# Fused score tiles accumulated in parts, and matmuls on zeros ahead of the first load: talking-heads attention and a squared-ReLU feed-forward in one kernel

## Chip, cores and metric

The kernel runs on one core of one Trainium2 chip. The metric is the device time of one execution in microseconds (us). Before the change the median of three runs is 600.85 us (600.27 to 602.12). One execution more was profiled; it took 600.99 us, and its trace, from the first instruction to the last, spans 599.2 us. Engines are named as in the profile: PE is TensorE (matmuls), PEld its weight loads, DVE VectorE, ACT ScalarE, POOL GpSimd, and SP the engine whose queue issues most DMAs.

## What is computed

Eight batches, 12 heads, 448 positions, head size 64. Scores are mixed over the heads before the softmax, and the attention weights are mixed again after it. The result is the input of a feed-forward of 768 to 2048 to 768 with a squared ReLU.

```python
scores = scale * np.matmul(q, k.transpose(0, 1, 3, 2))
scores = np.einsum('bhij,hg->bgij', scores, w_pre)
scores = scores - np.max(scores, axis=-1, keepdims=True)
attn = np.exp(scores)
attn = attn / (np.sum(attn, axis=-1, keepdims=True) + 1e-09)
attn = np.einsum('bhij,hg->bgij', attn, w_post)
attn_out = np.matmul(attn, v)
x = attn_out.transpose(0, 2, 1, 3).reshape(B * S, H * D)
h = np.maximum(x @ w_in, 0.0)
out = h * h @ w_out
```

## The kernel before, in words

**Tiles and steps.** A step is one tile: 10 query positions (`IQ`) of one batch with all 12 heads, 120 rows (`RG`). A batch has 45 tiles (`NT`), so there are 360 steps. At step i, `mix` (L369) makes the mixed scores of tile i in a PSUM bank `m_ps`, ACT takes the exp with its row sum (L384), DVE the reciprocal (L386), POOL the scaled second mixing matrix `pn` (L388). Four steps later (`LAG`) `unmix` (L392) multiplies the exps with `pn` on PE (L401), and DVE copies the result to `at` (L403). Between these, feed-forward units fill PE's time.

**Two ways to a mixed tile.** From tile 12 of batch 0 on, the plain scores of 120 or 128 queries, a block, are made by a burst (`score_burst`, L320): for each of the pairs of heads two matmuls into `s_ps` banks (L332), copied to the S tile by ACT (L342) or DVE (L344). There are two S tiles, so a block overwrites the one of two blocks before. `gather` (L349) then brings the rows of 10 queries with all heads together in a G tile with a DMA on SP's queue (L361), and one matmul of `mix` (L381) mixes the heads. The first 12 tiles of batch 0 (`FUSED`) have no S: there `mix_queries` (L172) has multiplied the turned queries with the mixing weights on DVE (L176; the products, named `w` in the profile, lie in the room of the later w_out weights), and `mix` makes the tile with six accumulating matmuls (L376), one for each pair of heads.

**The start.** q and k of batch 0 come in three loads each of four heads (q0, k0, q1, k1, q2, k2 below), issued on POOL's queue (L83), then v. `turn_unit` (L181) turns four heads with 16 transposes on PE (L193) and one copy (L195): queries on DVE, keys on ACT. For each unit u the order is: turn q, mix the first `NEAR` = 4 tiles' queries and then the other eight, turn k. After unit 1 the burst of pairs 0 and 1 of block (0,0) is made (in the order written). Pairs 2 and 3 follow in step 0, pairs 4 and 5 in step 1. From step 2 (`GATHERS_AT`) two gathers a step are written, from tile 12 on, until all 12 tiles of the block are gathered; then one a step, 10 tiles ahead (`AHEAD`). Some gathers bring the next block's bursts along: those of tiles 17 and 20 the bursts of block (0,1), those of tiles 29 and 32 (steps 19 and 22) those of block (0,2), which takes the S tile of block (0,0).

**What sets the order.** PE's and POOL's instructions run in the order of the program (`manual_schedule`, L425). On ACT, DVE and SP a scheduler orders them when the kernel is built. All eight PSUM banks are one pool: `tr_ps`, `s_ps`, `m_ps`, `at_ps`, `h_ps`, `o_ps` and `ot_ps` take one each and give it back when it has been read.

**Loads at steps.** POOL issues the loads of weights and of the next batches at fixed steps, each ahead of that step's `pn`: w_in at -1, 1, 3, 18, 21 and 24 (`W1_AT`), batch 1's k and q at 5, 7, 9, 11, 13 and 15 (`KQ_AT`).

```python
if h % 2 == 0 or (b == 0 and h in ((1, 3) if blk == 0 else (3, 9))):
    nc.scalar.copy(out=sb[:, h, :], in_=ps[:, 0:S])
```

The two lines (L341) share a burst's copies out: of block (0,0)'s 12 copies ACT makes eight.

Of the kernel before, what the change touches and what calls it, by code (L numbers as in the profile page):

```python
# [8 lines left out]
BF16 = mybir.dt.bfloat16  # L9
# [5 lines left out]
B, H, S, D = 8, 12, 448, 64  # L15
DMODEL = H * D
DFF = 2048
NPAIR = H // 2
# [3 lines left out]
IQ = 10  # L22
NT = 45
RG = H * IQ
FUSED = 12
FQ = FUSED * IQ
NEAR = 4
STARTS = {0: (FQ, 2 * FQ, S - 128)}
FIRST = {0: (FUSED, 2 * FUSED, 3 * FUSED)}
BURSTS = {0: ([5, 8], [5, 8], [3, 6])}  # L30
for _b in range(1, B):
    STARTS[_b], FIRST[_b], BURSTS[_b] = (0, 128, 256, 384), (0, 13, 26, 39), ([5, 8], [5, 8], [6], [0, 3])
GATHERS_AT = 2
HALF = H // 2
TT = 15
TQ = TT * IQ
# [14 lines left out]
def kernel(  # L51
# [11 lines left out]
    nc = tc.nc  # L63
    P = nc.NUM_PARTITIONS

    consts = ctx.enter_context(tc.tile_pool(name="consts", bufs=1))
# [7 lines left out]
    def bank(name, dtype=F32):  # L74
        return psp.tile([P, 512 if dtype == F32 else 1024], dtype, name=name, tag="ps")
# [6 lines left out]
    def load(t, src, b, h0=0, h1=H):  # L82
        nc.gpsimd.dma_start(out=t[0:PR, h0:h1, :, :].rearrange("p h r d -> p h (r d)"),  # L83
                            in_=src[b, h0:h1, :, :].rearrange("h (p r) d -> p h (r d)", r=R))

    staged, vs = {}, {}
    staged[0] = (stage_tile("qst", 1), stage_tile("kst", 1))
# [41 lines left out]
    for t in range(3 * P // IQ, NT):  # L129
        n0, n = max(0, 3 * P - IQ * t), min(IQ, S - IQ * t)  # L130
# [29 lines left out]
    for t in ets:  # L160
# [4 lines left out]
    w2 = [wts.tile([P, FT // 4, DMODEL], BF16, name=f"w2_{x}") for x in range(4)]  # L165

    qTs, kTs, xts, h2ts, ats = {}, {}, {}, {}, {}

    qmix = [w2[u][:, :, :].rearrange("p c m -> p (c m)")[:, 0:2 * FQ * H].rearrange(
        "p (y t g i) -> p y t g i", y=2, g=H, i=IQ) for u in range(NPAIR // 2)]  # L170

    def mix_queries(u, t0, t1):  # L172

        for y in range(2):
            qs = qTs[0][:, 2 * u + y, IQ * t0:IQ * t1].rearrange("p (t i) -> p t i", i=IQ)
            nc.vector.tensor_tensor(out=qmix[u][:, y, t0:t1, :, :],  # L176
                                    in0=qs.unsqueeze(2).to_broadcast([P, t1 - t0, H, IQ]),
                                    in1=wrep[:, 2 * u + y, :, :].unsqueeze(1).to_broadcast([P, t1 - t0, H, IQ]),
                                    op=ALU.mult)
# [41 lines left out]
    def load_v(b, x):  # L221
        if x == 0:
            vs[b] = stage_tile("v", 2)
        load(vs[b], v, b, 4 * x, 4 * x + 4)
# [121 lines left out]
    def rows_of(t):  # L346
        return H * min(IQ, S - IQ * t)

    def gather(s):  # L349
# [16 lines left out]
            x += n  # L366
        Gs[s] = g

    def mix(s):  # L369
        n = rows_of(s[1])  # L370
        b, t = s
        ps = bank("m_ps")
        fused = b == 0 and t < FUSED
        if fused:
            for p in range(NPAIR):
                nc.tensor.matmul(ps[0:n, 0:S], rhs=kTs[b][:, p, :],  # L376
                                 lhsT=qmix[p // 2][:, p % 2, t, :, :].rearrange("p g i -> p (g i)"),
                                 start=(p == 0), stop=(p == NPAIR - 1))
        else:
            m = pres[max(x for x in pres if x <= t)] if b else pre  # L380
            nc.tensor.matmul(ps[0:n, 0:S], lhsT=m[0:n, 0:n], rhs=Gs.pop(s)[0:n, :], start=True, stop=True)  # L381
        e = ets[(NT * s[0] + s[1]) % ND]
        sm = work.tile([P, 1], F32, name="sm", tag="sm", bufs=4)
        nc.scalar.activation(out=e[0:n, 0:S], in_=ps[0:n, 0:S], func=ACT.Exp, scale=SCALE, accum_out=sm[0:n, 0:1])  # L384
        rc = work.tile([P, 1], F32, name="rc", tag="rc", bufs=4)
        nc.vector.reciprocal(out=rc[0:n, :], in_=sm[0:n, :])  # L386
        pn = work.tile([P, RG], BF16, name="pn", tag="pn", bufs=LAG + 2)
        nc.gpsimd.tensor_scalar(out=pn[0:n, :], in0=(post_gi if fused else post)[0:n, :], scalar1=rc[0:n, 0:1], scalar2=1.0,  # L388
                                op0=ALU.mult, op1=ALU.mult)
        esb[s] = (e, pn)  # L390
# [20 lines left out]
    def at_step(i, unit):  # L411
        timed.setdefault(i, []).append(unit)
# [10 lines left out]
    blocks = [(b, blk) for b in range(B) for blk in range(len(STARTS[b]))]  # L423
    steps = [(b, t) for b in range(B) for t in range(NT)]
    with tc.manual_schedule(engines={PE, POOL}):  # L425
        for x in range(3):
            load_v(0, x)
        for u in range(NPAIR // 2):
            turn_unit(0, 0, u)
            mix_queries(u, 0, NEAR)  # L430
            mix_queries(u, NEAR, FUSED)
            turn_unit(0, 1, u, nc.scalar.copy)
            if u == 1:
                score_burst(0, 0, [0, 1])
        loads = {}
        ahead = [FUSED]

        def at_load(i, f, *args):
            loads.setdefault(i, []).append(lambda: f(*args))

        for x in range(3):
            at_load(V1_AT[x], load_v, 1, x)
        for x in range(6):
            at_load(KQ_AT[1][x], load_qk, 1, x)
            at_load(KQ_AT[2][x], load_qk, 2, x)
        for x, i in enumerate(W1_AT):
            at_load(i, load_w1, x)
        for x, i in enumerate(W2_AT):
            at_load(i, load_w2, x)
        for b in range(1, B):  # L450
            if b + 2 < B:
                for x in range(6):
                    at_load(NT * b + (30 if b == 1 else 22) + 2 * x, load_qk, b + 2, x)
            if b + 1 < B:
                for x in range(3):
                    at_load(NT * b + 34 + 2 * x, load_v, b + 1, x)
        def begin(units):
            owed[0] = max(owed[0], 0.0)
            filler.extend(units)

        for x, third, q0, q1 in EARLY:
            at_step(x, (0, lambda third=third, q0=q0, q1=q1: begin(ffn1_third(third, q0, q1))))
        bounds = sorted({x[0] for x in EARLY} | {FFN2_AT, 2 * NT + 1 + LAG})
        end = len(steps) + LAG + 3
        for i in range(-1, end):
            for f in loads.get(i, []):
                f()
            if i < 0:
                continue
            if i == NT // 2:  # L470
                for (_, n), (t, order) in orders.items():
                    half_pre(n, t, order)
            s0 = steps[i] if i < len(steps) else None
            s1 = steps[i - LAG] if LAG <= i < len(steps) + LAG else None
            if s0:
                b, t = s0
                if t == 0:
                    if b + 1 < B:
                        for x, u in enumerate(turn_units(b + 1)):
                            at_step(i + TURN.get(b, TURN[B])[x], u)  # L480
            early = [x for x in bounds if x > i]
            rest = early[0] - i if early else (1 + LAG - i) % NT + 1
            rest = min(rest, end - i) if i > len(steps) - NT // 2 else rest
            share = sum(w for w, _ in filler) / rest / 2
            now = timed.pop(i, [])
            if s0:
                mix(s0)
            for w, f in now:
                f()
                owed[0] -= w  # L490
            fill(share)
            if s1:
                unmix(s1)
                b1, t1 = s1
                if t1 % TT == TT - 1:
                    for u in av_units(b1, t1 // TT):
                        at_step(i + 3, u)
                if t1 == NT - 1:
                    at_step(i + 3 if b1 else FFN2_AT, (0, lambda b1=b1: filler.extend(ffn_units(b1))))
            if i < 2:  # L500
                score_burst(0, 0, [2 + 2 * i, 3 + 2 * i])
            for _ in range(2 if i >= GATHERS_AT else 0):
                if ahead[0] > min(max(i + AHEAD, 2 * FUSED - 1), len(steps) - 1):
                    break
                b2, t2 = steps[ahead[0]]
                gather((b2, t2))
                ahead[0] += 1
                blk2 = max(x for x in range(len(FIRST[b2])) if FIRST[b2][x] <= t2)
                nxt = blocks.index((b2, blk2)) + 1
                first = BURSTS[b2][blk2]  # L510
                if nxt < len(blocks) and t2 - FIRST[b2][blk2] in first:
                    x = first.index(t2 - FIRST[b2][blk2])
                    score_burst(*blocks[nxt], [3 * x, 3 * x + 1, 3 * x + 2])
            if i + 1 < end:
                fill(share)
        for j in sorted(timed):
            for _, f in timed[j]:
                f()
        fill(1e12)
# [30 lines left out]
```

## Time and profile before

| what | value |
|---|---|
| median of three runs | 600.85 us |
| profiled execution, and its span | 600.99 us, 599.2 us |
| DVE, ACT, POOL busy, of the span | 69%, 64%, 54% |
| granted clock, mean of the span | 0.995 |
| PE idle before its first matmul | 7.12 us |
| L376, the fused tiles' matmuls, 24 to 40 us | x42, 355 ns each |
| L401 (unmix), whole span | x1440, 216 ns each |
| L251 and L295 (feed-forward), whole span | x960, 315 ns; x768, 326 ns |
| gathers (G<-S), 105.0 KB | x284 |
| DMA, mean over the span | 121 GB/s |

The spans of matmuls overlap, since they are pipelined; a row "x6" in the timeline gives the length of six together. An engine's idle time counts where the chain that ended last goes through it. Each digit of the page's slices is a fortieth of the span, 15 us; DMA stands for how busy the core's 16 DMA engines were:

```profile
PEclk9999999999999999999999999999999999999999
DMA  9898999698569755795458855697544755431003
GB/s 128 141 199 164 191 197 196 128 172 193 100 101 140 145 100 109 121 156 124 98 94 135 151 111 101 113 143 138 109 79 69 133 119 107 84 50 54 27 27 79
```

### The profile page before, as it was taken

What the parts mean: (1) busy time and instruction counts of PE and PEld (TensorE: products, weight loads), DVE (VectorE), ACT (ScalarE), POOL (GpSimd) and SP (SyncE); (2) the same over time, 40 slices, a digit from 0 to 9 for tenths busy, and PEclk for the clock granted to TensorE, in tenths of its full rate; (3) what the DMA queues carried; (4) which work ended last, traced back from release to release, by engine and by line L of the source; (5) the groups of instructions that cost most, each with busy time, mean ns of one, the idle gap of its engine ahead of it and who ended that gap; (6) DMA issues with size and microseconds to landing.
All of it is one profiled execution on the core that took longest, in us unless ns stands there. A gap on an engine that the chain in (4) does not pass through costs nothing.

```text
span 599.2 us, 17220 instructions
## 1 busy us (share of the span) xinstructions
PE 574.3 (96%) x6011; PEld 372.2 (62%) x6011; DVE 411.7 (69%) x1044; ACT 380.6 (64%) x1105; POOL 326.1 (54%) x708
## 2 busy tenths in 40 slices
PE   4979999899999999999999999999999999999996
PEld 3547777566566666566565665666665666666553
DVE  5668769988767777767777777777867667666011
ACT  3757978676876557864776547775677547762410
POOL 5354897362777227862569316792377325761730
PEclk9999999999999999999999999999999999999999
DMA  9898999698569755795458855697544755431003
GB/s 128 141 199 164 191 197 196 128 172 193 100 101 140 145 100 109 121 156 124 98 94 135 151 111 101 113 143 138 109 79 69 133 119 107 84 50 54 27 27 79
DMA packets 88279, 72.28 MB, mean 121 GB/s; under 512 B 6688, under 2 KB 83200, under 8 KB 88192
## 3 DMA queue, kind: packets, MB, share of 16 engines
q1 hardware_dynamic: 50394, 48.16, 36.6%
q0 software_dynamic: 37216, 22.81, 29.3%
q8 instruction: 47, 0.77, 0.5%
q10 hardware_dynamic: 582, 0.21, 0.2%
q14 instruction: 40, 0.33, 0.1%
HBM read 45.70 MB, written 11.01 MB: 95 GB/s over the span
## 4 chain that ended last, share of the span: by engine, by line
PE 81%; DMA 10%; ACT 3%; issue 2%; DVE 1%; POOL 1%; SPq 1%; ACTq 0%; POOLq 0%; DVEq 0%
PE o_ps L295 24%; PE h_ps L251 22%; PE at_ps L401 10%; PE m_ps L381 10%; DMA G<-S 7%; PE ot_ps L209 6%; PE s_ps L332 4%; PE tr_ps L193 3%; ACT e L384 2%; DMA w<-in_moe_w_in_dram 2%; DMA kst<-in_k_dram 1%; ACT S L342 1%; PE m_ps L376 1%; DVE S L344 1%; PE s_ps L338 1%
## 5 line engine op out<-in xcount | busy, mean ns | idle before, releaser
L403 DVE CAST at<-at_ps 112x480 bf16<-112x480 f32 x360 | 228.5, 650 | 73.3 <-PE at_ps L401 72.8
L384 ACT ACTIVATE e<-m_ps 120x448 bf16<-120x448 f32 x360 | 195.5, 547 | 98.8 <-PE m_ps L381 92.4
L388 POOL TENSOR_SCALAR pn<-post,rc 120x120 bf16<-120x120 bf16 x348 | 129.0, 372 | 207.1 <-DVE rc L386 147.6
L251 PE MATMUL h_ps<-xt,w 128*128 128x448 bf16 (+2 forms) x960 | 169.6, 315 | 1.1 <-ACT hr L257 0.6
L295 PE MATMUL o_ps<-w,h 128*128 128x384 bf16 x768 | 138.7, 326 | 0.3 <-ACT S L342 0.2
L401 PE MATMUL at_ps<-pn,e 120*128 120x120 bf16 (+1 forms) x1440 | 135.1, 216 | 0.7 <-POOL pn L388 0.5
L401 PEld LDWEIGHTS <-e 120*128 120x128 bf16 (+1 forms) x1440 | 103.9, 98 | 45.0 <-issue 1.4
L381 PE MATMUL m_ps<-G,pre 120*120 120x448 bf16 x348 | 124.6, 358 | 2.1 <-ACT S L342 1.0
L251 PEld LDWEIGHTS <-w 128*128 128x128 bf16 x960 | 84.6, 98 | 57.7 <-issue 5.6
L262 POOL TENSOR_TENSOR h<-hr 128x384 bf16<-128x384 f32 (+1 forms) x144 | 106.1, 738 | 19.4 <-ACT hr L257 15.6
L257 ACT ACTIVATE hr<-h_ps 128x448 f32<-128x448 f32 (+2 forms) x160 | 75.4, 473 | 52.7 <-PE h_ps L251 35.9
L295 PEld LDWEIGHTS <-h 128*128 128x128 bf16 x768 | 72.8, 98 | 48.2 <-issue 5.5
L344 DVE CAST S<-s_ps 128x448 bf16<-128x448 f32 x159 | 89.2, 615 | 4.2 <-DMA G<-S 2.3
L386 DVE RECIPROCAL rc<-sm 120x1 f32<-120x1 f32 x360 | 57.2, 159 | 45.2 <-ACT e L384 37.3
L342 ACT CAST S<-s_ps 128x448 bf16<-128x448 f32 x171 | 79.8, 546 | 11.9 <-PE s_ps L332 8.4
L384 ACT ACTIVATION_READ_ACCUMULATOR e<-m_ps 120x1 f32 x360 | 74.1, 206 | 0.0
L304 DVE COPY osb<-o_ps 128x384 f32<-128x384 f32 x54 | 30.1, 557 | 46.8 <-PE o_ps L295 46.6
L381 PEld LDWEIGHTS <-pre 120*120 120x120 bf16 x348 | 46.1, 133 | 20.9 <-issue 14.6
L332 PE MATMUL s_ps<-kT,qT 64*128 64x448 bf16 x288 | 41.5, 355 | 5.8 <-ACT S L342 4.4
L209 PE MATMUL ot_ps<-at,v 112*64 112x150 bf16 x1152 | 42.6, 230 | 0.0
L209 PEld LDWEIGHTS <-v 112*64 112x64 bf16 x1152 | 38.3, 110 | 4.9 <-issue 4.9
L215 ACT CAST xt<-ot_ps 128x450 bf16<-128x450 f32 (+1 forms) x48 | 25.5, 533 | 20.4 <-PE ot_ps L209 19.9
(45 smaller groups left out, 288.2 us busy)
## 6 DMA issues: line engine op xcount, KB each, us to landing
G<-S SPq DMA_DIRECT2D x284, 105.0 KB
qst<-in_q_dram POOLq DMA_DIRECT2D x24, 224.0 KB, 5.7
kst<-in_k_dram POOLq DMA_DIRECT2D x24, 224.0 KB, 5.2
v<-in_v_dram POOLq DMA_DIRECT2D x24, 224.0 KB, 6.9
G<-S SPq DMA_DIRECT2D x70, 52.5 KB
w<-in_moe_w_in_dram POOLq DMA_DIRECT2D x6, 512.0 KB, 10.3
w<-in_moe_w_out_dram POOLq DMA_DIRECT2D x8, 384.0 KB, 7.7
out_dram<-osb SPq DMA_DIRECT2D x8, 336.0 KB
```

The costliest lines, as they stand in the source:

```text
L209: nc.tensor.matmul(ps[64 * hh:64 * hh + 64, TQ * y:TQ * y + TQ], lhsT=vs[b][0:PR, g, r, :], rhs=at[0:PR, r, g, :], start=(y == 0 and r == ...
L251: nc.tensor.matmul(ps[:, 0:n], lhsT=w1[ft // 8][:, c2, ft % 8 * 128:ft % 8 * 128 + 128], rhs=xts[b][:, c2, n0:n1], start=(c2 == 0), stop=( ...
L257: nc.scalar.activation(out=hr[:, 0:n], in_=ps[:, 0:n], func=ACT.Relu)
L262: eng.tensor_tensor(out=dst[:, x - o:y - o], in0=hr[:, x - n0:y - n0], in1=hr[:, x - n0:y - n0], op=ALU.mult)
L295: nc.tensor.matmul(ps[:, 0:384], lhsT=lhsT, rhs=w2[ft // 4][:, ft % 4, nt * 384:(nt + 1) * 384], start=(ft == 0), stop=(ft == FT - 1))
L342: nc.scalar.copy(out=sb[:, h, :], in_=ps[:, 0:S])
L344: nc.vector.tensor_copy(out=sb[:, h, :], in_=ps[:, 0:S])
L381: nc.tensor.matmul(ps[0:n, 0:S], lhsT=m[0:n, 0:n], rhs=Gs.pop(s)[0:n, :], start=True, stop=True)
L384: nc.scalar.activation(out=e[0:n, 0:S], in_=ps[0:n, 0:S], func=ACT.Exp, scale=SCALE, accum_out=sm[0:n, 0:1])
L388: nc.gpsimd.tensor_scalar(out=pn[0:n, :], in0=(post_gi if fused else post)[0:n, :], scalar1=rc[0:n, 0:1], scalar2=1.0, op0=ALU.mult, op1=A ...
L401: nc.tensor.matmul(ps[:, RG * r:RG * r + RG], lhsT=e[0:n, PR * r:PR * r + P], rhs=pn[0:n, :], start=True, stop=True)
L403: nc.vector.tensor_copy(out=ats[(b, third)][0:PR, :, :, IQ * tl:IQ * tl + IQ], in_=ps[0:PR, 0:R * RG].rearrange("p (r g i) -> p r g i", r= ...
```

## The change

Two matters are changed. First, PE runs 13 matmuls of 512 columns on a zeroed tile at the start of its program, and two more after the first keys are turned (`still`, `WARM`); a memset on DVE makes the tile, and one PSUM bank takes the results, which nothing reads. Second, the first five fused tiles (`NEAR` = 5) get their `m_ps` bank while the heads are turned, and their six matmuls come in three parts of two, one for each unit of four heads (`fused_part`): the parts of units 0 and 1 stand between the turning of q and of k of the next unit, and the last part is made by `mix`. `mix` calls the same function for the other fused tiles, which get all three parts at their step.

With that the burst of pairs 0 and 1 moves from unit 1 of the start to step 0, those of pairs 2 and 3 and of pairs 4 and 5 each one step later, and the gathers start at step 4. So the gathers of tiles 17 and 20, and the bursts of block (0,1) with them, come at steps 6 and 8 and no longer at 4 and 6. `mixed` gives the same addresses as `qmix` did.

```diff
-NEAR = 4
+NEAR = 5
-GATHERS_AT = 2
+GATHERS_AT = 4
+WARM = (13, 2)
...
+    still_in = consts.tile([P, 512], BF16, name="still_in")
+    nc.vector.memset(still_in[:, :], 0.0)
+    still_out = bank("still_ps")
+
+    def still(n):
+        for _ in range(n):
+            nc.tensor.matmul(still_out[:, :], lhsT=still_in[:, 0:P], rhs=still_in[:, :], start=True, stop=True)
...
-    qmix = [w2[u][:, :, :].rearrange("p c m -> p (c m)")[:, 0:2 * FQ * H].rearrange(
-        "p (y t g i) -> p y t g i", y=2, g=H, i=IQ) for u in range(NPAIR // 2)]
+    def mixed(u, y, t0, t1):
+        x = RG * (FUSED * y + t0)
+        return w2[u][:, :, :].rearrange("p c m -> p (c m)")[:, x:x + RG * (t1 - t0)]
...
-            nc.vector.tensor_tensor(out=qmix[u][:, y, t0:t1, :, :],
+            nc.vector.tensor_tensor(out=mixed(u, y, t0, t1).rearrange("p (t g i) -> p t g i", g=H, i=IQ),
...
+    parts = {}
+
+    def fused_part(t, u):
+
+        if t not in parts:
+            parts[t] = [0, bank("m_ps")]
+        if parts[t][0] > u:
+            return
+        parts[t][0] = u + 1
+        for p in (2 * u, 2 * u + 1):
+            nc.tensor.matmul(parts[t][1][0:RG, 0:S], rhs=kTs[0][:, p, :], lhsT=mixed(u, p % 2, t, t + 1),
+                             start=(p == 0), stop=(p == NPAIR - 1))
+
     def mix(s):
...
-        ps = bank("m_ps")
         fused = b == 0 and t < FUSED
         if fused:
-            for p in range(NPAIR):
-                nc.tensor.matmul(ps[0:n, 0:S], rhs=kTs[b][:, p, :],
-                                 lhsT=qmix[p // 2][:, p % 2, t, :, :].rearrange("p g i -> p (g i)"),
-                                 start=(p == 0), stop=(p == NPAIR - 1))
+            for u in range(NPAIR // 2):
+                fused_part(t, u)
+            ps = parts[t][1]
         else:
+            ps = bank("m_ps")
...
     with tc.manual_schedule(engines={PE, POOL}):
+        still(WARM[0])
...
             mix_queries(u, NEAR, FUSED)
+            if u:
+                for t in range(NEAR):
+                    fused_part(t, u - 1)
             turn_unit(0, 1, u, nc.scalar.copy)
-            if u == 1:
-                score_burst(0, 0, [0, 1])
+            if u == 0:
+                still(WARM[1])
...
-            if i < 2:
-                score_burst(0, 0, [2 + 2 * i, 3 + 2 * i])
+            if i < 3:
+                score_burst(0, 0, [2 * i, 2 * i + 1])
```

## The prediction, made before the result was known

> **What bounds the kernel now.** I read the busy table first: TensorE (PE) works 574.3 us of a span of 599.2 us, so the whole kernel has 25 us in which it stands still. The stretch view (bounds in us and length; busy time and count of PE, weight loads, DVE, ACT, POOL; granted clock, DMA share, GB/s) tells where.
>
> ```profile
> PE 574.3 (96%) x6011; PEld 372.2 (62%) x6011; DVE 411.7 (69%) x1044; ACT 380.6 (64%) x1105; POOL 326.1 (54%) x708
> ...
> 0.00:5.00 5.00, 0.00 (x0) 0.00 (x0) 0.95 (x8) 1.28 (x1) 3.79 (x10) 1.00 0.27 37
> ...
> 40.00:45.00 5.00, 1.44 (x9) 0.76 (x6) 2.63 (x7) 1.88 (x5) 1.01 (x3) 0.92 1.16 208
> ...
> 200.00:250.00 50.00, 49.65 (x542) 32.12 (x541) 37.81 (x93) 33.38 (x97) 24.72 (x56) 1.00 0.60 111
> ```
>
> After 150 us PE is busy 49.6 to 49.9 of every 50 us: whatever the start loses or gains is carried to the end. Of the 25 us, 7.12 pass before the first q lands, 3.5 lie between 40.2 and 43.7, and about 5 in the tail. The timeline (start, length, engine, line) shows the start that the change rebuilds.
>
> ```profile
> 7.12 0.96 PE L193 MATMUL tr_ps<-ident,qst 112*64 112x112 bf16 x16 [7.12 <-DMA qst<-in_q_dram]
> 11.64 0.96 PE L193 MATMUL tr_ps<-ident,kst 112*64 112x112 bf16 x16 [0.21 <-DMA kst<-in_k_dram]
> 13.44 1.85 ACT L342 CAST S<-s_ps 128x448 bf16<-128x448 f32 x4
> 15.03 2.24 PE L376 MATMUL m_ps<-kT,w 128*120 128x448 bf16 x6
> 17.30 0.55 ACT L384 ACTIVATE e<-m_ps 120x448 bf16<-120x448 f32 x1 [1.20 <-PE m_ps L376]
> 17.68 1.35 PE L376 MATMUL m_ps<-kT,w 128*120 128x448 bf16 x6
> 20.70 19.28 SPq L361 DMA_DIRECT2D G<-S  x17
> ```
>
> The rows of one kind change their length at 16.9 us (six L376 matmuls 2.24, then 1.35; 16 transposes 0.96, later 0.58): until then the clock is at half. S of block (0,0) is complete at 20.61 and its gathers start at 20.70. The chain of waits tells why that matters:
>
> ```profile
> 23.64 9.95 DMA G<-S
> 33.59 0.02 issue
> 33.60 9.42 DMA G<-S
> 43.02 0.02 issue
> ```
>
> The fourth gather is issued at 23.64 and lands at 33.59; the twelfth, which uses the same completion semaphore, is then issued and lands at 43.02. Only then may block (0,2) overwrite that S buffer: its burst, reached by PE at 39.27 in step 19, can't be copied, so that after five of its six matmuls no PSUM bank is free and PE stops at 40.2 (3.47 us). After it the clock drops to half for 44.2 to 47.6, which costs another 1.7 us of work. So in the first 45 us the end is set by gathers, not by PE.
>
> **The change, part by part.**
>
> *Zero matmuls.* Six cold 448-column matmuls took 2.24 us, 0.373 each, so 512 columns take about 0.43 us and 13 take 5.5: from about 1.2 (after a memset of 0.2 to 0.5 us, by the 0.22 us of the ident memset) to 6.8. The wait for q until 7.12 hides all of it; without that cover it would cost 5.5. The two more (0.43 us warm) lie behind k's transposes, ahead of q's second landing at 10.43. I take the clock as full from 7 us on; the other bound, half until 15 us, is a rival.
>
> *NEAR 5.* L176 took 405 ns for 480 elements and 653 for 960; on that line 600 and 840 take 467 and 591, the same sum (1.058 us): nothing. The address rewrite is nothing either.
>
> *Parts.* The matmuls stay 30 for five tiles; 20 move ahead of the last k transposes, in two groups of ten. A warm one costs 0.192 us (18 rows: 3.62, last latency 0.355), so a group is 1.95 us. But PE takes its work in program order, and each group waits for a kT copy (ACT, 0.91 us) and holds back the next k transposes: k0 lands 9.25, is turned by 9.87, copied by 10.8. q1's transposes end 11.05; group one ends 13.0; k1 (landed 11.60) is turned by 13.55 instead of 12.60, copied 14.5; group two ends 16.5; k2 (landed 13.95) is turned by 17.1 instead of 15.1, copied 18.05; the last two matmuls of tile 0 end 18.65. Its exp starts at **18.7 instead of 17.30**. This is where the warm clock's gain goes.
>
> *The burst.* The four s_ps of pairs 0 and 1, copied by ACT at 13.44 in time that was idle, now stand behind exp 0. All eight ACT copies of block (0,0) (0.46 us each) and three exps (0.54 before the next) are then in one queue: 18.7 + 3 x 0.54 + 8 x 0.46 = **24.0 instead of 20.61**. DVE's four copies (0.62) run beside them. Five banks held by the parts leave three for a burst of four; the fourth waits for exp 0 (about 0.3 us of PE), later ones for the copies, inside the same ACT queue. Two further exps slipping ahead would give 25.1; fewer than these three cannot stand ahead.
>
> *Starting gathers at step 4.* It puts the first gather's place behind the last burst; SP waits for S anyway, so the issue is at about 24.1. The bursts of block (0,1) move from steps 4 and 6 to 6 and 8 without more work. PE is then at step 5 at 24.3 (before: 23.87) with 0.8 us of burst still to do, and comes to step 19 at about 40.4 instead of 39.27, still ahead of its gathers: no cost of its own.
>
> *The DMA steps carried along.* w_in's third load waits in POOL's queue behind tile 2's pn: issue 24.05 instead of 22.06. The packets of the trace, summed by queue, say what this does: from 25 to 30 us (third w_in load, 2048-byte packets) the load queue moved 492 KB and the gather queue 74 KB; from 30 to 43 they shared, gathers 97 KB a us. A gather is 105 KB. Before the starved stretch, gathers had 215 KB through (23 to 25.2); first packets come 2.4 us after the first issue, so now at 26.5, into that load.
>
> *Sum.* If both legs of the chain keep their lengths, the twelfth lands 3.4 us later, 46.4. If the load is through its slow stretch 5.5 us after its start at about 25.5, and the 215 KB are missing, I come to 46.2. If half the load is through before the first gather packet arrives, 44.5. If gathers are not starved at all: 26.5 + 430/97 = 31 for the fourth, and 9.42 more, 40.4. I take 45.4, nearer to the legs as measured: **2.4 us later than 43.02**, the half-clock stretch after it stays, PE work after it is the same, and the profiled 600.99 us (span 599.2 and 1.8 around it; the median of the runs, 600.85, is 0.14 below) become **603.4**.
>
> **A rule weighed.** The rows between 10.07 and 13.49 show PE 88% busy, three quarters of it with transposes, and the clock still half; between 44.2 and 47.6, with half of it transposes, the clock opened. The Trainium skill, "TensorE: Matmul & The Clock Gate", Part 1, says that a window of 3.4 us of sustained work opens the clock and an idle one closes it; Part 4 there says that transposes do not count as PE work. By Part 1 the zero matmuls open it by 7 us, and 603.4 stays; by Part 4 the stretch from 6.8 to 10.5 would count as idle and close it again (the rival below). The second stretch of the trace speaks for the first.
>
> **Rivals.**
>
> *Clock half at the parts.* A group of ten takes 3.73 us and 16 transposes 0.96: k0 and q1 are turned 0.4 us later, group one ends at 15.1, k1 copied 17, and with the clock open from there the first exp comes at 20.9 instead of 18.7. The gathers follow: 603.4 + 2.2 = 605.6. For it: PE will be idle for 1.6 us between 7.7 and 9.3. Against: the idle time before the drop at 44.2 was 3.5.
>
> *Gathers without starvation: faster.* If w_in's load is through when the gathers come, the fourth lands by 31 and the twelfth at 40.4 to 41.5, as PE comes to step 19. The stall shrinks from 3.5 us to about 1, too short for the clock to fall: 600.99 - 2 - 1.7 = 597.3; from a landing at about 42 on it decides. For it: w_in's second load, alone, moved 193 KB in the microsecond from 22. Against: each w_in load began with packets of 0.8 to 1.6 us, gathers starved again at 57 to 59 us under another. "DMA: Bandwidth & Descriptors" of the Trainium skill, Queues, rings and completion order, has engines alternating between queues packet by packet; packets from 36 to 42 agree (some 200 to 115, over 16 and 10 engines), those from 25 to 30 do not (381 to 90).
>
> *Later slack swallows it.* A landing at 44 or less, or 1.1 us back at 114.4, where PE waits 1.12 for a q load: 601.5. For it: loads go on during the stall. Against: the load queue ran dry at 54 us and waited for a POOL issue, which shifts with the steps.
>
> **Chances.** Forecast 0.48; half clock 0.12; no starvation 0.19; swallowed 0.21. A difference under 0.3% (1.8 us) can't be told from none. A sixth of the forecast's cases come out under 1.8, some of the swallowed ones over it: slower 0.59, same 0.22, faster 0.19. The range runs from a half-realised no-starvation case, 598.6, to just over the half clock's, 606.2; the forecast's own is 602.4 to 604.6.
>
> **What would show it.** Right: slow rows gone by 8 us; first L384 near 18.7; first L361 near 24; PE idle ending near 46, slow rows for 3.4 us after. Wrong: first L361 before 22.5, the S buffer's release before 43, or PE's step 19 not waiting at all.

## The result, and the profile after

The changed kernel takes 603.55 us in the median of 20 runs (600.69 to 606.68); the kernel before, in 20 runs beside it, 600.86 us. The ratio is 1.0042, with a 95% interval of 1.0026 to 1.0057: 2.7 us slower, and the interval does not hold 1. The profiled execution took 602.83 us, with a span of 601.0, against 600.99 and 599.2.

The busy table and the stretch view of the changed kernel (columns as before):

```profile
PE 578.4 (96%) x6026; PEld 372.5 (62%) x6026; DVE 412.6 (69%) x1045; ACT 380.2 (63%) x1105; POOL 326.6 (54%) x708
...
0.00:5.00 5.00, 3.80 (x12) 1.44 (x13) 1.00 (x8) 1.28 (x1) 3.79 (x11) 1.00 0.27 36
20.00:25.00 5.00, 4.37 (x21) 1.42 (x21) 2.06 (x6) 4.37 (x14) 1.42 (x3) 1.00 0.28 22
40.00:45.00 5.00, 2.30 (x30) 1.20 (x24) 4.45 (x12) 2.25 (x8) 3.43 (x8) 1.00 1.15 191
200.00:250.00 50.00, 49.41 (x541) 31.96 (x540) 37.97 (x92) 33.27 (x96) 23.70 (x54) 1.00 0.60 110
```

The stretch from 20 to 25 us in the kernel before:

```profile
20.00:25.00 5.00, 5.00 (x33) 3.19 (x31) 2.63 (x9) 3.73 (x12) 2.49 (x6) 1.00 0.95 154
```

PE's greater busy time (4.1 us) is the zero matmuls, 4.39 and 0.60 us of them, not more work. From 20 to 25 us the DMA engines now stand nearly still, 22 GB/s instead of 154: the gathers have not begun, and w_in's second load stands in POOL's queue behind tile 0's `pn`. The timeline of the start of the changed kernel:

```profile
1.20 4.39 PE L93 MATMUL still_ps<-still_in 128*128 128x512 bf16 x13 [1.20 <-DVE still_in L88]
...
7.23 0.58 PE L203 MATMUL tr_ps<-ident,qst 112*64 112x112 bf16 x16 [1.65 <-DMA qst<-in_q_dram]
9.75 0.58 PE L203 MATMUL tr_ps<-ident,kst 112*64 112x112 bf16 x16 [1.93 <-DMA kst<-in_k_dram]
10.92 0.96 PE L203 MATMUL tr_ps<-ident,qst 112*64 112x112 bf16 x16
11.81 3.32 PE L389 MATMUL m_ps<-kT,w 128*120 128x448 bf16 x10
15.06 0.58 PE L203 MATMUL tr_ps<-ident,kst 112*64 112x112 bf16 x16
...
16.65 2.05 PE L389 MATMUL m_ps<-kT,w 128*120 128x448 bf16 x10 [0.61 <-ACT kT L205]
18.63 0.58 PE L203 MATMUL tr_ps<-ident,kst 112*64 112x112 bf16 x16
20.21 0.54 PE L389 MATMUL m_ps<-kT,w 128*120 128x448 bf16 x2 [1.00 <-ACT kT L205]
...
20.79 0.54 ACT L406 ACTIVATE e<-m_ps 120x448 bf16<-120x448 f32 x1 [0.63 <-PE m_ps L389]
...
25.96 6.71 SPq L371 DMA_DIRECT2D G<-S  x7
```

The zero matmuls opened the clock (transposes of 0.58 us at 7.23), but by the records of the granted clock it was half again from 10.9 to 14.3, just under the first group of ten: 3.32 us instead of 2.05. Each group waits for a kT copy and holds back the next k transposes, as the prediction said. The first exp comes at 20.79 (before 17.30), the first gather at 25.96 (20.70), and the twelfth lands at 44.20 (43.02). Here and below a gather's landing is the last of the eleven updates that it makes to its completion semaphore in the trace. PE's two stops after that, in steps 19 and 29, where block (0,2) takes the S tile of (0,0) and block (1,0) that of (0,1):

```profile
44.88 0.41 PE L342 MATMUL s_ps<-kT,qT 64*128 64x448 bf16 x1 [2.43 <-ACT S L352]
...
59.16 0.35 PE L342 MATMUL s_ps<-kT,qT 64*128 64x448 bf16 x1 [1.27 <-ACT S L352]
```

In the kernel before, the second stop was small (and the first 3.47):

```profile
57.42 0.35 PE L332 MATMUL s_ps<-kT,qT 64*128 64x448 bf16 x1 [0.57 <-ACT S L342]
```

The first stop ends later, since the twelfth gather lands later, and is shorter all the same, since PE itself comes to step 19 only at 41.7 (39.3). G of tile 35, the last gather from block (0,1), lands at 58.28 instead of 56.54, and the first tile of batch 1 is mixed at 78.49 instead of 77.01. From there to the end it is 522.5 against 522.2 us.

### The profile page after: what moved, and what is told of

It reads as the page before. It is cut to its first block, busy times and chain, and to the rows that moved or that the text cites. A ratio compares the mean times of both kernels' runs of the same rounds, so it can differ in the third digit from the quotient of the medians.

```text
span 601.0 us, 17250 instructions
## 1 busy us (share of the span) xinstructions
PE 578.4 (96%) x6026; PEld 372.5 (62%) x6026; DVE 412.6 (69%) x1045; ACT 380.2 (63%) x1105; POOL 326.6 (54%) x708
## 4 chain that ended last, share of the span: by engine, by line
PE 86%; DMA 5%; ACT 4%; issue 2%; POOL 1%; DVE 1%; SPq 0%; ACTq 0%; DVEq 0%; POOLq 0%
PE o_ps L305 25%; PE h_ps L261 23%; PE at_ps L423 11%; PE m_ps L403 10%; PE ot_ps L219 6%; PE s_ps L342 4%; DMA G<-S 4%; PE tr_ps L203 3%; PE m_ps L389 3%; ACT S L352 2%; ACT e L406 2%; DMA qst<-in_q_dram 1%; PE s_ps L348 1%; POOL h L272 0%; DVE at L425 0%
## 5 line engine op out<-in xcount | busy, mean ns | idle before, releaser
L403 PEld LDWEIGHTS <-pre 120*120 120x120 bf16 x348 | 46.2, 133 | 19.9 <-issue 10.1
L219 PE MATMUL ot_ps<-at,v 112*64 112x150 bf16 x1152 | 42.4, 229 | 0.0
L225 ACT CAST xt<-ot_ps 128x450 bf16<-128x450 f32 (+1 forms) x48 | 25.4, 534 | 20.0 <-PE ot_ps L219 19.4
```

What stands on the lines that cost most here:

```text
L219: nc.tensor.matmul(ps[64 * hh:64 * hh + 64, TQ * y:TQ * y + TQ], lhsT=vs[b][0:PR, g, r, :], rhs=at[0:PR, r, g, :], start=(y == 0 and r == ...
```

## Experiments

Twelve kernels, each with at least six runs and beside runs of the kernel before. One profile each stands behind every trace time below; ratios are to the kernel before. The table gives, from each trace: the first gather's issue, the landing of the last gather from block (0,0) (tile 23) and from (0,1) (tile 35), the first mixed tile of batch 1, and the span.

| kernel | first gather | tile 23 | tile 35 | batch 1 | span | ratio and interval |
|---|---|---|---|---|---|---|
| before | 20.70 | 43.02 | 56.54 | 77.0 | 599.2 | 1 |
| changed | 25.96 | 44.20 | 58.28 | 78.5 | 601.0 | 1.0042 (1.0026 to 1.0057) |
| before, zeros alone | 21.17 | 42.84 | 56.64 | 76.8 | 599.0 | 1.0027 (1.0001 to 1.0052) |
| changed, no zeros | 26.66 | 44.90 | 59.91 | 80.1 | 604.8 | 1.0036 (1.0013 to 1.0060) |
| changed, clock held | 25.41 | 44.28 | 57.65 | 78.9 | 601.3 | 1.0014 (0.9992 to 1.0036) |
| changed, k first | 23.80 | 42.43 | 56.27 | 76.5 | 598.5 | 1.0009 (0.9985 to 1.0034) |
| before, third load late | 21.10 | 38.70 | 60.49 | 82.3 | 605.7 | 1.0090 (1.0063 to 1.0117) |
| changed, third load late | 25.50 | 43.03 | 59.72 | 81.4 | 605.0 | 1.0136 (1.0093 to 1.0179) |
| changed, gathers at 2 | 25.13 | 43.13 | 59.93 | 81.4 | 603.1 | 1.0055 (1.0033 to 1.0077) |
| changed, burst early | 23.45 | 45.22 | 58.72 | 79.0 | 603.8 | 1.0042 (1.0017 to 1.0068) |
| changed, second load early | 27.05 | 45.27 | 59.15 | 79.3 | 601.4 | 1.0037 (1.0019 to 1.0054) |
| changed, both loads early | 26.76 | 46.19 | 59.16 | 81.2 | 605.0 | 1.0065 (1.0039 to 1.0091) |
| before, both loads early | 20.53 | 37.12 | 56.79 | 78.1 | 600.6 | 1.0043 (1.0026 to 1.0061) |
| k first, both loads early | 23.22 | 40.76 | 55.19 | 75.4 | 597.9 | 1.0019 (0.9995 to 1.0044) |

**The zero matmuls alone**, in the kernel before.

```diff
+        still(13)
...
+            if u == 0:
+                still(2)
             if u == 1:
                 score_burst(0, 0, [0, 1])
```

> The kernel before, with the 13 and 2 zero matmuls alone. Theory (the end of the start is set by when the gathers of block (0,0) start and how fast they go): full clock from about 4 us gives 16 transposes in 0.58 us and tile 0's six matmuls in 1.3 instead of 2.24, but q and k land when they did; k2, landed at 13.95, is copied by 15.5, the first exp moves from 17.30 to 16.8, the first gather from 20.70 to about 20.2, the release of the S buffer from 43.0 to 42.5: 0.5 us faster at most (ratio 0.998 to 1.000). Rival (half clock itself is what the start pays for): 2 us or more faster (0.997 or less). Rival (the zero matmuls are the cost): slower, 1.003 or more.

Measured 601.61 against 600.47 us, ratio 1.0027. Neither the 2 us of the half-clock rival nor the theory's half microsecond came. But in the profile the clock was half again from 7.7 to 14.5 us, and the first exp came at 17.77, so this run did not take the half clock away and can't decide on that rival. The gathers and the span are those of before, so the slower median has no cause in this trace, and its interval almost reaches 1.

**The change without them.**

```diff
-WARM = (13, 2)
+WARM = (0, 0)
```

> The changed kernel without zero matmuls. In the profiled run of the changed kernel the clock was open from 4.1 to 10.9 us and half again to 14.3, so that the first group of ten took 3.3 us. Theory (late S and late gathers): without them the group is as slow and the transposes before it too; first exp at 21 instead of 20.8, first gather at 26 to 26.5; time as the changed kernel's, 1.003 to 1.006 against before. Rival (zero matmuls hold a good part of the change up): 1.008 or more. Rival (zero matmuls cost): 1.002 or less.

603.10 us, ratio 1.0036, the theory's band: no sign that the zero matmuls hold a good part of the change up or cause its loss, though the interval leaves room for some of either. First exp 21.48, first gather 26.66, both a little later than expected. The span of 604.8 has a second cause, a half-clock stretch from 122.0 to 125.4; the stretch view shows it as granted clock:

```profile
120.00:126.00 6.00, 4.81 (x23) 2.61 (x23) 4.00 (x9) 2.64 (x8) 1.46 (x3) 0.72 0.64 89
```

**The clock held at full** with eight more zero matmuls while PE waits for k0.

```diff
             mix_queries(u, NEAR, FUSED)
+            if u == 0:
+                still(8)
```

> The changed kernel with eight more zero matmuls after q0 is turned, in the 1.9 us in which PE stood idle before k0; the clock should then stay full from 4 us on. Rival of the prediction (the clock at half at the parts is what costs): group one takes 1.95 to 2.1 instead of 3.3 us, first exp at 18.9, first gather at 24.2, and the loss against before goes to 0.5 us or less (ratio 1.001 or less). Theory (the moved burst and ACT's queue make the gathers late even so): gathers still start 3.4 us later than before, the release lies at 43.3 to 44, ratio 1.001 to 1.004.

```profile
8.24 1.90 PE L93 MATMUL still_ps<-still_in 128*128 128x512 bf16 x8
10.80 0.58 PE L203 MATMUL tr_ps<-ident,kst 112*64 112x112 bf16 x16 [0.66 <-DMA kst<-in_k_dram]
...
12.48 2.10 PE L389 MATMUL m_ps<-kT,w 128*120 128x448 bf16 x10
...
20.23 0.54 ACT L406 ACTIVATE e<-m_ps 120x448 bf16<-120x448 f32 x1 [0.63 <-PE m_ps L389]
```

The clock stayed full from 6.0 to 43.6 us and the group took 2.10. But k0 landed late in this execution (10.8, against 9.75 with the change), so the first exp was only 0.6 us earlier, not 1.9. 602.00 us, ratio 1.0014, in the theory's band and near its lower end: by the ratios the dip may cost 1.7 us of the 2.7, but the interval overlaps with that of the change, and the trace shows no gain (the twelfth gather lands at 44.28, the first tile of batch 1 is mixed at 78.9). What the dip costs stays open.

**k turned ahead of the parts.**

```diff
+            turn_unit(0, 1, u, nc.scalar.copy)
             if u:
                 for t in range(NEAR):
                     fused_part(t, u - 1)
-            turn_unit(0, 1, u, nc.scalar.copy)
```

> The changed kernel with the parts behind the turning of the same unit's k instead of ahead of it: same work, other order. Theory (groups of ten hold back k's transposes and with them kT's copies): k1 is turned by 12.9 instead of 15.6 and k2 by 16 instead of 19.2; first exp at about 18.6 instead of 20.8, first gather at 23.8 instead of 26.0, release earlier by 1 to 2 us; ratio to before 1.000 to 1.003. Rival (order on PE is no matter, ACT's copies and exps alone set the gathers' start): first gather at 25 or later, ratio as the changed kernel's, 1.003 to 1.006.

```profile
11.96 0.96 PE L203 MATMUL tr_ps<-ident,kst 112*64 112x112 bf16 x16
12.85 2.42 PE L389 MATMUL m_ps<-kT,w 128*120 128x448 bf16 x10
...
15.62 0.56 PE L203 MATMUL tr_ps<-ident,kst 112*64 112x112 bf16 x16
...
18.62 0.54 ACT L406 ACTIVATE e<-m_ps 120x448 bf16<-120x448 f32 x1 [1.50 <-PE m_ps L389]
...
23.80 6.83 SPq L371 DMA_DIRECT2D G<-S  x7
```

Same work, other order, and every time came out as expected: k1 turned by 12.9, k2 by 16.2, first exp 18.62, first gather 23.80, tile 23's gather 1.8 us earlier than with the change. 601.67 us, ratio 1.0009: the interval holds 1, and by the ratios about three quarters of the loss is gone. The two intervals still touch, from 1.0026 to 1.0034; taken as independent, they put the difference at 0.0033, give or take 0.0029 (an estimate), so some gain is fairly sure and its size is not. The clock dip, 10.1 to 13.5, is in this profile too.

**The third w_in load at step 16**, in the kernel before and in the changed one.

```diff
-W1_AT = (-1, 1, 3, 18, 21, 24)
+W1_AT = (-1, 1, 16, 18, 21, 24)
```

> The kernel before, with the third w_in load issued at step 16 instead of step 3, so that none of the w_in loads runs while the twelve gathers of block (0,0) do. Theory (the release of that S tile, which stops PE, is late because the gathers are starved under that load from 25 to 30 us): the third gather lands near 27 instead of 32.5, the twelfth at 38 to 40 instead of 43.0, PE's 3.5 us stop in step 19 is gone or under 1 us, and so is the half-clock stretch after it: 3 to 5 us faster, ratio 0.991 to 0.995. Rival (gathers go at a pace of their own): the twelfth lands at 42 or later, ratio 0.998 to 1.002. Rival (the load is then late for the feed-forward at 54.8): a new wait there, ratio above 1.002.

> The changed kernel with the third w_in load at step 16. Theory: first gather still at 26, but the twelfth lands at 41 to 42 instead of 44.2, as PE comes to step 19 at 41.7; stop under 1 us, no half clock after it: 2.5 to 4 us faster than the changed kernel, ratio to before 0.998 to 1.001. Against the kernel before with the same late load it stays 2 us or more slower, since PE itself comes to step 19 some 2.4 us later. Rival (the start of the gathers alone counts, not the load): as the changed kernel, 1.003 to 1.006.

Both went the other way: 606.81 us (1.0090) and 609.01 us (1.0136). In the kernel before, the part up to step 19 was as expected: third gather at 26.8, twelfth at 38.70, no stop in step 19. But four w_in loads, issued from 39 to 49 us, now followed each other beside the gathers of block (0,1), and the stop came back larger in step 29, as 9.13 us:

```profile
61.37 0.53 PE L332 MATMUL s_ps<-kT,qT 64*128 64x448 bf16 x1 [9.13 <-ACT S L342]
```

In the changed kernel the twelfth gather gained only 1.2 us, and the gather of tile 35 came 1.4 us later.

**Gathers written from step 2.**

```diff
-GATHERS_AT = 4
+GATHERS_AT = 2
```

> The changed kernel with gathers written from step 2, as before the change; the bursts of block (0,1) go back to steps 4 and 6 with them. Theory (SP waits for S, the written place costs nothing): first gather at 25.5 to 26.5 as with the change, ratio to before 1.003 to 1.006. Rival (the two steps' delay of the gathers is the cost): first gather near 24, ratio 1.002 or less.

603.83 us, 1.0055: no gain, so the written place of the gathers is not the cost. The first gather at 25.13 is 0.8 us earlier than with the change. In this profile the stop in step 29 is 5.4 us: the twelfth gather lands at 43.13, as in the kernel before (43.02), and the span is 3.9 us longer all the same, behind a tile 35 that lands 3.4 us later.

**The burst of pairs 0 and 1 back at unit 1**, with three tiles in parts.

```diff
-NEAR = 5
-GATHERS_AT = 4
+NEAR = 3
+GATHERS_AT = 2
...
             if u == 0:
                 still(WARM[1])
+            if u == 1:
+                score_burst(0, 0, [0, 1])
...
-            if i < 3:
-                score_burst(0, 0, [2 * i, 2 * i + 1])
+            if i < 2:
+                score_burst(0, 0, [2 + 2 * i, 3 + 2 * i])
```

> The changed kernel with the burst of pairs 0 and 1 back behind unit 1 and the other two back at steps 0 and 1, gathers from step 2, and three fused tiles in parts instead of five, so that the PSUM banks suffice. Theory (the moved burst puts eight copies and three exps into one ACT queue behind exp 0): S of block (0,0) is complete at 22.5 to 23.5 instead of 25.9, though the first exp stays near 20, and the release is 1 to 2 us earlier than with the change; ratio to before 1.000 to 1.003. Rival (the parts' order on PE is the whole cost): first gather at 25 or later, ratio 1.003 to 1.006.

S was complete at 23.4, as expected, and the first exp at 20.54. But the release came at 45.2, not 1 to 2 us earlier: the first gathers met w_in's third load, issued 1.1 us behind the first of them, and the third gather landed only at 35.2. Ratio 1.0042, as the change and in the rival's band, though the rival's first gather at 25 or later did not come. S was 2.5 us earlier than with the change, and alone that gained nothing.

**w_in loads issued early**: the second alone, or the second and third, right behind the first.

```diff
-W1_AT = (-1, 1, 3, 18, 21, 24)
+W1_AT = (-1, -1, 3, 18, 21, 24)
```

> The changed kernel with the second w_in load issued right behind the first instead of at step 1, where it waits in POOL's queue for tile 0's pn. With the change the DMA engines moved 22 GB/s from 20 to 25 us (before: 154). Theory (that idle stretch is the loss: the same bytes must be through before the S tiles of blocks (0,0) and (0,1) are released to steps 19 and 29): the load fills the stretch, the releases come 1 to 2 us earlier, ratio to before 1.000 to 1.003. Rival (late first exp, PE and ACT alone): as with the change, 1.003 to 1.006.

```diff
-W1_AT = (-1, 1, 3, 18, 21, 24)
+W1_AT = (-1, -1, -1, 18, 21, 24)
```

> The changed kernel with the second and third w_in loads right behind the first, so that both are through by about 24 us, before the first gather packet. Theory (idle DMA stretch, then gathers starved under the third load): twelfth gather by 42, PE's stop in step 19 under 1 us and none in step 29; 3 to 4 us faster than the changed kernel, ratio to before 0.997 to 1.000. Rival (the stop only moves to step 29, as with the late load): ratio 1.003 or more. Rival (late first exp): 1.003 to 1.006.

> The kernel before with the second and third w_in loads right behind the first. Before the change the DMA engines had little idle time at that place (19 to 20 us), but the third load ran beside the gathers. Theory: twelfth gather at 39 to 41 instead of 43.0, no w_in load moved nearer to the later gathers, so no stop in step 29 either; 2 to 5 us faster, ratio 0.992 to 0.997. Rival (there is no idle DMA time to fill, so nothing to gain; the stop moves on): 0.998 to 1.002.

> The changed kernel with k turned ahead of the parts and with the second and third w_in loads right behind the first. Theory: both mended, first gather near 24, no stop in step 19; ratio 0.994 to 0.998. If the parts and the full clock are worth anything, this one is level with or faster than the kernel before with the same loads; if they only delay S, it is 0.001 to 0.003 slower than that one.

Four misses. With the second load early (603.54 us, 1.0037) the idle stretch of the DMA engines only moved, to 23 to 28 us, since the third load and the gathers still waited for exps; with both early (605.45 us, 1.0065) it lay at 24 to 28, and the twelve gathers, with no w_in load beside them, took 19.4 us from the first issue to the last landing (18.2 with the change). So the third load is not what makes them slow there. In the kernel before (603.38 us, 1.0043) the gathers of block (0,0) were through at 37.12 and the stop in step 19 was gone, but tile 35's gather, issued 5 us earlier than before, landed at the same time (56.79), and PE stood in step 29 instead:

```profile
57.67 0.53 PE L332 MATMUL s_ps<-kT,qT 64*128 64x448 bf16 x1 [6.00 <-ACT S L342]
```

From 54.0 on the clock was half for 6.8 us. With k first, both loads early give 601.70 us, 1.0019: by the median better than both loads early in the change as it is (the intervals just touch), not faster than the kernel before, and not to be told from k first alone. Against the kernel before with the same loads (1.0043) it is level or better, and the intervals overlap.

## Why the prediction was right, step by step

**The time** (603.4 forecast, 603.55 measured) and the sign were right, but terms of the sum were off in opposite senses: the first gather came 1.9 us later than worked out, and the way from there to the release was 3.1 us shorter. That the time came out within 0.2 us is luck.

*Zero matmuls.* Hidden by the wait for q, as said: they ended at 5.6 us. The price by row was right (0.43 us cold each). "The clock as full from 7 us on" failed: in nine of the ten profiles with zero matmuls the clock was half again by 7.7 to 10.9 us for one or two stretches of 3.4; only the one with eight more kept it. That was the first rival, given 0.12. It is most of why the first exp came at 20.79, close to that rival's 20.9, and not 18.7: the first group of ten took 3.32 us instead of 1.95, and it began at 11.81 instead of 11.05, since k0 came 0.5 us later (9.75) and q1's transposes ran at half clock (0.96 us). The rival's 605.6 did not come, because the legs below were shorter.

*Parts and order.* Right, and the best supported step: turning k first brought 18.62 and 23.80, and with them, by the medians, most of the time. How much of this loss the clock dip shares in is not settled: k first with the clock held was not run.

*The burst in ACT's queue.* From the first exp to the first gather 5.4 us were worked out and 5.2 measured (20.79 to 25.96). Alone it is not the whole cause, as the early burst shows.

*The legs of the gather chain.* This step was mis-sized: 21.3 us from the first issue to the release (24.1 to 45.4) were forecast, 18.2 measured. The release came 1.2 us later than before, not 2.4. From the first issue to the fourth landing it was 9.6 us (12.9 before), from there to the twelfth 8.7 (9.4). w_in's third load was issued at 26.06, not 24.05, only 0.1 us behind the first gather; from 28 to 32 us the gather queue moved 126 KB beside it, and then about 100 a us. No run changed this alone. (The 492 KB that the prediction gives to that load from 25 to 30 us were 403 of it and 89 of batch 1's k, in 512-byte packets.) Over the changed kernels with the loads at their old steps and the burst at step 0 the release follows the first gather: 23.80 to 42.4, 25.1 to 43.1, 25.4 to 44.3, 26.0 to 44.2, 26.7 to 44.9; the early burst, 23.45 to 45.2, is the exception.

*"Whatever the start loses is carried to the end."* Right after 80 us, but I ended the start at step 19. The late and early loads showed a second gate: no kernel gets past step 29 before tile 35's gather is in, and the first tile of batch 1 follows that landing by 20.2 to 20.5 us in eight of the fourteen profiles, and by 21.3 to 22.1 in those in which the clock fell on the way or PE itself came later than the gather. By that landing the DMA engines had moved 9.0 to 9.2 MB in ten of the fourteen profiles and 8.9 in another; in three with loads moved or a long second stop it was 9.6 to 9.7. That hints at the bytes ahead of it as what sets the second gate, which no run tested. In the changed kernel the second gate is 1.74 us later than before, its span 1.83. In the kernel before both gates bind almost together, which is why opening the first alone (38.70, 37.12) gained nothing. The rival "gathers without starvation: faster" had its premise met there, and its result failed for this reason.

*What is left.* The median lost 2.7 us, the profiled execution 1.8. The changed kernel's runs follow their mean granted clock (correlation -0.91: 0.997 in the fastest, 0.981 to 0.990 in the five slowest). Profiles of five variants show a further half-clock stretch between 118 and 127 us, and from batch 1's first tile to the end these took 523.4 to 524.8 us where the others took 521.7 to 522.5. That the change brings such stretches more often is possible but not shown.

## What to carry to other kernels

Interleaved work that has to wait for one unit's copy must not stand in front of the next unit's transposes on an in-order engine: turning k first, with the same instructions, took most of the loss away here, by the medians. When a buffer's release sets the end, look for the next release behind it before pricing the first, since a load moved out of one gate's way may stand in the next one's. Matmuls that keep the clock open have to go on until the real work is dense; a few microseconds of them at the start were lost again in the first gap in nine profiles of ten.

## What the runs showed of the hardware

A window about half idle is enough to halve the clock. The granted clock changes only at the ends of windows of 3.41 us (after the change it is full from 4.08 to 10.91, two steps, half to 14.32, one, and full to 45.04, nine). The Trainium skill, "TensorE: Matmul & The Clock Gate", Part 1, names an idle window as what closes it; by these traces a window that is about half idle does. Idle time alone is no exact measure: without zeros, PE stood still for 1.75 us of the window from 57.13 to 60.55 and the clock stayed, and for 1.47 of the window from 118.57 to 121.98 and it fell.

The columns that the matmuls streamed, by the trace's records, tell such windows apart (a matmul of 448 columns counts 448). The fourteen traces, up to 580 us, have 16 windows without transposes that began at full clock and lost it: none streamed more than 3918 columns. The 1986 such windows that kept it streamed 4068 or more. At 0.192 us for 448 columns a window has room for about 7,960, so the bound is near half of that (an estimate). A column of a transpose counts for less: four windows of 4400 to 4992 columns lost the clock, 1792 to 2688 of them in transposes, among them 39.75 to 43.16 with k first and both loads early. It still counts for something: 5888 columns, 3584 of them in transposes, kept the clock from 112.44 to 115.86 in the kernel before.

The same load landed at different times from one execution to the next: k0's first transposes began between 9.13 and 10.80 us, a spread of 1.7 us.
